# Reading x of the first three batches through column-tiled matmuls as it was loaded, with a new order of the loading phase

## The chip, the cores and the metric

The kernel runs on one core of a Trainium2 chip. The metric is the device time of one execution in microseconds (us); the median over several runs is compared. Engines, as the profile names them: PE is the matrix engine (TensorE, with PEld for its weight loads), DVE is VectorE, ACT is ScalarE, POOL is GpSimd, SP is SyncE, which here only issues DMAs. Each engine works through its own instructions in the order in which the program gives them.

## The reference

There are 8 batches of 8 heads, with 512 token rows and 32 state rows of 64 features. Tokens attend to the states and the states attend to the tokens; the 544 rows of each batch then go through a gated feed-forward block (512 to 1536 to 512).

```python
scores  = scale * x @ state.T ;  a  = exp(scores - max);  a  /= a.sum(-1) + 1e-9
xread   = a @ state                                   # for the 512 token rows
scores2 = scale * state @ x.T ;  a2 = exp(scores2 - max); a2 /= a2.sum(-1) + 1e-9
sread   = a2 @ x                                      # for the 32 state rows
y = concat([xread, sread], rows) ; heads side by side: 4352 x 512
out = (sigmoid(y @ w_gate) * (y @ w_val)) @ w_out     # float32
```

## The kernel before

One exponential table per batch, `E1` (128 token rows by 4 token groups c by 2 by 4 heads by 32 states), serves both directions. For the tokens, `n_sum`/`n_sums` and `n_mul`/`n_muls` divide it by its sum over the states, and its transpose `aT` (by `aT_mm` on PE for batches 0 and 1, by DMA later) is the moving operand of the block's first products. `xread` is never formed: the weights are first multiplied by the states (`sw_visit`, `sw_wide`: eight small matmuls at once on 64x32 tiles of the array, one per head, into PSUM, then `sw_cp` casts them to the SBUF tile `SW`), and `gv_mm(b, f)` multiplies `SW` by `aT` for one slice f of 128 of the 1536 hidden columns, gate and value half in a PSUM buffer each. `gv_th` (tanh on ACT) and `gv_glu` (product on DVE) form the gated slice and free those buffers; `out_mm(b, k)` sums four of twelve slices into 128 output rows.

For the states, `at_Eb` casts `E1` to bf16 (`Eb`, on POOL), and x is multiplied by it. Two ways of doing this exist. In batches 0 to 2 `sr_mm` (line 252) takes x in token order (`xb`, cast by `cast_x`) as the stationary operand, 16 matmuls of 64 columns; the sums over tokens come from eight matmuls with `ones` in batch 0, and in batches 1 and 2 from sums folded ahead by `p_tok`, `n_add` and `p_fold` and one matmul with `pick`; `sr_fin` divides and writes `XS`, the state rows of the block. In batches 3 to 7 `rd_mm` (line 285) takes `Eb` as stationary operand, 32 columns a head, four heads side by side on column tiles of the array, and `xs`, a copy of x with a column of ones, as the moving one: 32 matmuls of 65 columns; `rd_fin` divides and `rd_dma` transposes the result into `XS` by a DMA on SP. The block on the state rows of all batches, b = 8, comes last, from about 194 us on.

Loading: batch 0 comes partly as float32 (`load_xp`, then cast) and partly cast to bf16 by the DMA (`load_xh`, tile `xh`); batch 1 as `xh`; batches 2 on as float32. `load_w(w, lo, n)` loads columns lo to lo + n of the gate (0) or value (1) weights, cast on the way, `load_wo` the output weights, `load_sb` two batches of states. These go through POOL's queue. `xT_mm`/`xT_cp` transpose x for the scores `S_mm`, `S_exp` takes the exponential. `warm` issues matmuls whose result nobody reads.

PSUM has eight buffers: `GV` two, `SWP` four, `OU` one, `AT` one; a buffer is taken again when its last reader is done. The order of all calls is written out by hand (`manual_schedule`): lines 477 to 733 are the loading phase, in which batches 0 and 1 are worked through as their inputs and weights land; the loop at line 734 then treats batch b with the output of b - 1 and the preparation of b + 1.

Of the kernel before, what the change touches and what calls it, by code (L numbers as in the profile page):

```python
# [16 lines left out]
def kernel(  # L17
# [36 lines left out]
    ones = wp.tile((128, 2, 128), BF, name="ones")  # L54
# [192 lines left out]
    def sr_parts(b):  # L247
        ps = held["sr", b]
        return (ps[:, 0:256].rearrange("p (j e n) -> p j e n", j=4, e=2),
                ps[:, 256:384].rearrange("p (j n) -> p j n", j=4))  # L250

    def sr_mm(b, place):
        Eb = Ebs[b]
        held["sr", b] = place[0].tile((128, 512), FP, name="srp", tag=place[1])
        sr, sm = sr_parts(b)
        if ("hl", b) in held:
            nc.tensor.matmul(sm, pick, held["hl", b], start=True, stop=True)
            terms = []
        else:
            terms = [(e, Eb[:, c, e]) for e in range(2) for c in range(4)]  # L260
        for i, (e, rhs) in enumerate(terms):
            nc.tensor.matmul(sm, ones[:, e], rhs, start=(i == 0), stop=(i == len(terms) - 1))
        for j in range(4):
            for c in range(4):
                nc.tensor.matmul(sr[:, j], xbs[b][:, c, 2 * j:2 * j + 2].rearrange("p h d -> p (h d)"),  # L265
                                 Eb[:, c, :, j], start=(c == 0), stop=(c == 3))

    def sr_inv(b):
        r2 = held["r2", b] = ap_.tile((128, 4, Ns), FP, name="r2")
        nc.vector.reciprocal(r2, sr_parts(b)[1])  # L270

    def sr_fin(b):
        if ("r2", b) not in held:
            sr_inv(b)
        sr, r2 = sr_parts(b)[0], held["r2", b]
        for e in range(2):
            rows = slice(e * 64, (e + 1) * 64)
            nc.vector.tensor_tensor(XS[rows, b], sr[rows, :, e], r2[rows], ALU.mult)

# [5 lines left out]
    def rd_mm(b):  # L285

        ps = AT[0].tile((128, 512), FP, name="rdp", tag=AT[1])
        rd = held["rd", b] = ps[:, :2 * D + 2].rearrange("p (e d) -> p e d", e=2)
        for e in range(2):
            for c in range(4):  # L290
                for j in range(4):
                    nc.tensor.matmul(rd[j * Ns:(j + 1) * Ns, e], Ebs[b][:, c, e, j], xs[:, c, 2 * j + e, :D + 1],  # L292
                                     start=(c == 0), stop=(c == 3))
# [91 lines left out]
    def out_mm(b, k, place=None):  # L385
# [431 lines left out]
```

## Time and profile before

| | |
|---|---|
| median of 3 runs | 223.96 us (223.51 to 224.49) |
| the profiled execution | 224.5 us, span of its instructions 222.7 us |
| mean granted clock | 0.992 |
| PE busy | 213.9 us (96% of the span) |
| DVE, ACT, POOL busy | 123.5, 129.2, 66.6 us |
| `gv_mm` (L363), `out_mm` (L394) on PE | 96.5 and 95.9 us |
| HBM read, written | 18.35 and 8.91 MB |

The page splits the span in 40 slices of 5.57 us; a digit is a busy share in tenths. A timeline row gives start, length, engine, line, operation, output and inputs, the shape, the number of instructions merged, and in brackets how long the engine sat idle before and what ended it. The chain of waits follows the work that ended last back to what released it; its rows give start and length.

### The profile page before, as it was taken

What the parts mean: (1) busy time and instruction counts of PE and PEld (TensorE: products, weight loads), DVE (VectorE), ACT (ScalarE), POOL (GpSimd) and SP (SyncE); (2) the same over time, 40 slices, a digit from 0 to 9 for tenths busy, and PEclk for the clock granted to TensorE, in tenths of its full rate; (3) what the DMA queues carried; (4) which work ended last, traced back from release to release, by engine and by line L of the source; (5) the groups of instructions that cost most, each with busy time, mean ns of one, the idle gap of its engine ahead of it and who ended that gap; (6) DMA issues with size and microseconds to landing.
All of it is one profiled execution on the core that took longest, in us unless ns stands there. A gap on an engine that the chain in (4) does not pass through costs nothing.

```text
span 222.7 us, 4790 instructions
## 1 busy us (share of the span) xinstructions
PE 213.9 (96%) x1839; PEld 107.4 (48%) x1862; DVE 123.5 (55%) x214; ACT 129.2 (58%) x243; POOL 66.6 (30%) x124
## 2 busy tenths in 40 slices
PE   8679999999999999999999999999999999999994
PEld 3554444544444444444444444444444444466744
DVE  3599989986467445744484448354754334422301
ACT  3398797627675667656674866666756444433311
POOL 6699498556341036001800072003200000000001
PEclk9799999999999999999999999999999999999999
DMA  6999996984598349924552206421122111211114
GB/s 152 158 202 248 244 177 106 151 224 132 134 260 260 61 74 281 199 47 142 169 149 69 101 0 97 130 70 45 47 74 77 49 50 53 66 69 49 50 29 113
DMA packets 40982, 26.75 MB, mean 120 GB/s; under 512 B 23456, under 2 KB 36768, under 8 KB 40960
## 3 DMA queue, kind: packets, MB, share of 16 engines
q1 hardware_dynamic: 31088, 18.33, 31.6%
q0 software_dynamic: 9584, 7.93, 21.1%
q8 instruction: 14, 0.23, 0.4%
q10 hardware_dynamic: 288, 0.20, 0.3%
q14 instruction: 8, 0.07, 0.1%
HBM read 18.35 MB, written 8.91 MB: 122 GB/s over the span
## 4 chain that ended last, share of the span: by engine, by line
PE 90%; ACT 3%; DMA 3%; DVE 1%; issue 1%; POOL 0%; POOLq 0%
PE outp L394 38%; PE gvp L363 37%; PE swp L311 5%; PE gvp L366 5%; DMA xf<-in_x_dram 3%; PE Sp L152 1%; PE outp L416 1%; ACT E L157 1%; DVE SW L349 1%; PE rdp L292 1%; ACT xT L134 1%; PE xTp L131 0%; ACT aT L241 0%; ACT SW L349 0%; PE srp L265 0%
## 5 line engine op out<-in xcount | busy, mean ns | idle before, releaser
L378 DVE SCALAR_TENSOR_TENSOR glu<-th,gvp 128x512 bf16<-128x512 f32 (+1 forms) x108 | 70.1, 656 | 79.0 <-ACT th L373 63.5
L394 PE MATMUL outp<-wo,glu 128*128 128x512 bf16 x373 | 95.9, 379 | 1.3 <-issue 0.2
L363 PE MATMUL gvp<-aT,SW 128*128 128x512 bf16 x384 | 96.5, 379 | 0.5 <-ACT aT L241 0.5
L373 ACT ACTIVATE th<-gvp 128x512 f32<-128x512 f32 (+1 forms) x108 | 61.9, 576 | 59.3 <-PE gvp L363 45.8
L394 PEld LDWEIGHTS <-glu 128*128 128x128 bf16 x396 | 37.8, 98 | 41.9 <-issue 0.4
L363 PEld LDWEIGHTS <-SW 128*128 128x128 bf16 x384 | 36.2, 98 | 45.1 <-issue 4.2
L349 ACT CAST SW<-swp 128x512 bf16<-128x512 f32 x70 | 39.0, 586 | 4.3 <-PE swp L311 3.5
L398 ACT ACTIVATE res<-outp 128x512 f32<-128x512 f32 x33 | 19.7, 597 | 17.7 <-PE outp L394 17.7
L103 POOL COPY pre<-th 128x1 f32<-128x1 f32 x5 | 0.9, 188 | 69.0 <-ACT th L373 69.0
L407 POOL DMA_DIRECT2D out_dram<-res x2 | 1.1, 537 | 59.7 <-ACT res L398 59.7
L349 DVE CAST SW<-swp 128x512 bf16<-128x512 f32 x26 | 17.2, 684 | 2.9 <-PE swp L311 2.9
L163 POOL CAST Eb<-E 128x256 bf16<-128x256 f32 x32 | 12.0, 418 | 10.9 <-ACT E L157 10.9
L115 POOL CAST xb<-xf 128x1024 bf16<-128x1024 f32 x11 | 11.2, 1041 | 4.0 <-DMA xf<-in_x_dram 3.2
L157 ACT ACTIVATE E<-Sp 128x512 f32<-128x512 f32 x16 | 9.6, 604 | 3.3 <-PE Sp L150 2.8
L283 POOL CAST xs<-xf 128x1024 bf16<-128x1024 f32 x10 | 10.2, 1044 | 0.0
L311 PE MATMUL swp<-wg,sTc 64*32 64x512 bf16 (+1 forms) x192 | 8.7, 327 | 0.0
L170 DVE TENSOR_REDUCE rs<-E 128x16 f32<-128x512 f32 x12 | 8.2, 680 | 0.5 <-ACT E L157 0.4
L224 DVE TENSOR_TENSOR ab<-E,ri 128x512 bf16<-128x512 f32 x11 | 8.2, 742 | 0.0
L311 PE MATMUL swp<-wv,sTc 64*32 64x512 bf16 (+1 forms) x192 | 7.5, 322 | 0.0
L311 PEld LDWEIGHTS <-sTc 64*32 64x32 bf16 x384 | 4.9, 91 | 5.2 <-issue 3.0
L366 PE MATMUL gvp<-XS,wg 128*128 128x256 bf16 x48 | 7.2, 273 | 0.0
L366 PE MATMUL gvp<-XS,wv 128*128 128x256 bf16 x48 | 7.2, 273 | 0.0
(88 smaller groups left out, 129.0 us busy)
## 6 DMA issues: line engine op xcount, KB each, us to landing
out_dram<-res SPq DMA_DIRECT2D x27, 256.0 KB, 3.2
xf<-in_x_dram SPq DMA_DIRECT2D x4, 1024.0 KB, 6.6
xf<-in_x_dram POOLq DMA_DIRECT2D x2, 1024.0 KB, 7.5
wo<-in_moe_w_out_dram POOLq DMA_DIRECT2D x3, 512.0 KB, 5.6
out_dram<-res SPq DMA_DIRECT2D x9, 128.0 KB, 1.9
wg<-in_moe_w_gate_dram POOLq DMA_DIRECT2D x2, 512.0 KB, 9.3
wv<-in_moe_w_val_dram POOLq DMA_DIRECT2D x2, 512.0 KB, 10.4
xf<-in_x_dram POOLq DMA_DIRECT2D x3, 256.0 KB, 6.6
```

Source lines behind the costliest of these rows:

```text
L115: cp(xbs[b].rearrange("p c h d -> p h c d")[:, lo:lo + n], (xhs if b in xhs else xfs)[b][:, lo:lo + n])
L157: nc.scalar.activation(E1s[b][:, :, :, 2 * i:2 * i + 2].rearrange("p c e j n -> p (c e) j n"), held["S", b, i].rearrange("p c e j n -> p ( ...
L163: nc.gpsimd.tensor_copy(Ebs[b][:, c], E1s[b][:, c])
L283: pool(xs.rearrange("p c h d -> p h c d")[:, lo:lo + n, :, :D], xfs[b][:, lo:lo + n])
L311: nc.tensor.matmul(pss[e][j * Ns:(j + 1) * Ns, o:o + n], sTc[rows, b, j] if b > 1 else sTd[rows, b, 2 * j + e, e], (wg, wv)[w][rows, j, lo ...
L349: cp(*sw_left.pop((b, lo, w, e)))
L363: nc.tensor.matmul(ps, SWs[b][:, g, w, fs], aTs[b][:, :, g], start=(g == 0), stop=(g == 1))
L366: nc.tensor.matmul(ps, (wg, wv)[w][:, j, fs], XS[:, :, j], start=(j == 0), stop=(j == 3))
L373: nc.scalar.activation(th, held["gv", b, f][0], AF.Tanh, scale=0.5)
L378: nc.vector.scalar_tensor_tensor(glus[b][:, f], held["th", b, f], 1.0, held["gv", b, f][1], ALU.add, ALU.mult)
L394: nc.tensor.matmul(ops[b, c], glus[b][:, f, c * 128:(c + 1) * 128], wo[:, f], start=(f == 0), stop=(f == NF - 1))
L398: nc.scalar.activation(res, ops[b, c], AF.Copy, scale=0.5)
```

## The change

`sr_mm`, `sr_fin`, `sr_inv`, `p_fold`, `p_tok`, `n_add` and the tile `pick` go. `rd_mm` serves all batches: for batches 0 to 2 its moving operand is x as it was loaded (`xh` in batches 0 and 1, `xb` in batch 2), 64 columns, and 32 further matmuls of one column with a tile of ones give the sums. Its PSUM buffer is now named by the caller. The casts of batches 0 and 1 to token order go with that. The result tile `xr` has four buffers, and the three `rd_dma` of batches 0 to 2 are issued in the loop at b = 2, f = 8. Output rows of batch 6 are stored in halves for the last group only. `warm` has a tile of its own, filled with zeros. The loading phase is ordered anew: other PSUM buffers, other engines for some casts and copies, another order of the loads (x of batch 1 ahead of all weights; the weight columns 512 to 1023 ahead of 0 to 255; x of batch 2 after all of them), and three `gv_mm` of batch 1 just ahead of the loop.

```diff
-ones = wp.tile((128, 2, 128), BF, name="ones")
+ones = wp.tile((128, 1), BF, name="ones")
+wm = wp.tile((128, 128), BF, name="wm")
...
-def rd_mm(b):
+def rd_mm(b, place):
...
+                h, o, Eb = 2 * j + e, rd[j * Ns:(j + 1) * Ns, e], Ebs[b][:, c, e, j]
+                if b > 2:
+                    nc.tensor.matmul(o, Eb, xs[:, c, h, :D + 1], start=(c == 0), stop=(c == 3))
+                else:
+                    xh = xhs[b][:, h, c] if b in xhs else xbs[b][:, c, h]
+                    nc.tensor.matmul(o[:, :D], Eb, xh, start=(c == 0), stop=(c == 3))
+        if b < 3:
+            for c in range(4):
+                for j in range(4):
+                    nc.tensor.matmul(rd[j * Ns:(j + 1) * Ns, e, D:], Ebs[b][:, c, e, j], ones, start=(c == 0), stop=(c == 3))
...
-    xr = held["xr", b] = ap_.tile((128, 2, D), BF, name="xr")
+    xr = held["xr", b] = ap_.tile((128, 2, D), BF, name="xr", bufs=4)
...
-            n = 256 if 4 * (B - 1) - 4 <= 4 * b + c < 4 * (B - 1) else 512
+            n = 256 if 4 * (B - 1) - 1 <= 4 * b + c < 4 * (B - 1) else 512
...
+            if b == 2 and f == 8:
+                for q in range(3):
+                    rd_dma(q)
```

The new order of the loading phase, cut:

```diff
+nc.vector.memset(wm, 0.0)
+warm(2, AT)
+warm(1, SWP)
+load_s(0, nc.scalar)
+warm(4, GV)
+load_xp(0, nc.sync, 0, 2)
+make_identity(nc, ident)
+warm(1, OU)
+warm(2, GV)
+load_xh(0, 4, 4)
+zero(sTd, vec)
+cast_xp(0, vec, 0, 2)
+cast_s(0, vec)
+xT_mm(0, 0, GV)
+sT_mm(0, GV)
+sT_pad(1, act)
+xT_cp(0, 0, vec)
+sT_pad(0, vec)
+load_xh(1, 0, 4)
+load_xp(0, nc.sync, 2, 2)
+cast_xp(0, act, 2, 2)
+xT_mm(0, 1, SWP)
+S_mm(0, 0, GV, (0,))
+xT_cp(0, 1, vec)
+S_mm(0, 0, OU, (1,))
+S_exp(0, 0)
+xT_mm(0, 2, GV)
+xT_cp(0, 2, vec)
+load_xh(1, 4, 4)
+xT_mm(0, 3, OU)
+load_w(0, 256, 256)
+xT_cp(0, 3, act)
+S_mm(0, 1, OU, (0,))
+S_mm(0, 1, GV, (1,))
+load_w(1, 256, 256)
+S_exp(0, 1)
+xT_mm(1, 0, GV, 2)
+n_sum(0, 0)
+zero(sbz, vec)
+load_w(0, 1024, 512)
+n_sum(0, 1)
+load_w(1, 1024, 512)
+n_mul(0, 0, pool)
+xT_cp(1, 0, act, 2)
+xT_mm(1, 2, OU, 2)
+at_Eb(0)
+n_mul(0, 1, vec)
+S_mm(1, 0, GV)
+S_exp(1, 0)
+xT_cp(1, 2, vec, 2)
+aT_mm(0, SWP)
+aT_cp(0, 0, act)
+nc.vector.memset(ones, 1.0)
+S_mm(1, 1, SWP)
+load_sb(1)
+S_exp(1, 1)
+sw_visit(0, 256, 256)
+aT_cp(0, 1, vec)
+sw_cp(0, 256, 2, 0, act)
+load_w(1, 512, 512)
+sw_cp(0, 256, 2, 1, vec)
+sw_visit(1, 256, 256)
+warm(2, OU)
+at_Eb(1)
+load_sb(3)
+n_sums(1)
+gv_mm(0, 2, SWP)
+gv_th(0, 2)
+gv_glu(0, 2)
+gv_mm(0, 3, GV)
+sw_cp(1, 256, 2, 1, act)
+load_sb(2)
+rd_mm(0, OU)
+gv_th(0, 3)
+n_muls(1, vec)
+gv_glu(0, 3)
+load_w(0, 512, 512)
+sw_cp(1, 256, 2, 0, act)
+sw_visit(1, 1024, 512, 0)
+sw_cp(1, 1024, 0, 0, act)
+sw_visit(0, 1024, 512, 0)
+sw_cp(0, 1024, 0, 1, act)
+sw_cp(0, 1024, 0, 0, act)
+aT_mm(1, GV)
+rd_mm(1, AT)
+sw_visit(0, 1024, 512, 1)
+sw_cp(1, 1024, 0, 1, act)
+load_w(1, 0, 256)
+aT_cp(1, None, vec)
+sw_cp(0, 1024, 1, 1, vec)
+sw_cp(0, 1024, 1, 0, act)
+sw_visit(1, 1024, 512, 1)
+sw_cp(1, 1024, 1, 1, vec)
+gv_mm(0, 8, GV)
+gv_th(0, 8)
+gv_glu(0, 8)
+gv_mm(0, 11, SWP)
+nc.gpsimd.memset(xs[:, :, :, D:], 1.0)
+rd_fin(1)
+sw_cp(1, 1024, 1, 0, act)
+gv_mm(1, 2, SWP)
+gv_th(0, 11)
+rd_fin(0)
+load_w(0, 0, 256)
+gv_th(1, 2)
+gv_glu(0, 11)
+gv_mm(1, 9, GV)
+gv_th(1, 9)
+gv_glu(1, 2)
+sw_visit(0, 512, 512, 1)
+sw_cp(0, 512, 1, 0, act)
+gv_glu(1, 9)
+gv_mm(1, 3, SWP)
+gv_mm(0, 10, GV)
+sw_cp(0, 512, 1, 1, vec)
+gv_th(1, 3)
+sT_mm(1, AT)
+gv_th(0, 10)
+sT_cp(1, act)
+gv_glu(1, 3)
+sw_visit(0, 512, 512, 0)
+sw_visit(1, 512, 512, 0)
...
+gv_glu(0, 10)
+sw_cp(0, 512, 0, 0, act)
+load_x(2, nc.gpsimd)
+load_wo(1)
+gv_mm(1, 11, GV)
+sT_mm(2, AT)
+sw_cp(1, 512, 0, 0, act)
+sT_mm(3, OU)
+sw_cp(0, 512, 0, 1, vec)
+sw_visit(0, 0, 256)
+sw_cp(1, 512, 0, 1, vec)
+sw_visit(1, 512, 512, 1)
+gv_th(1, 11)
+gv_glu(1, 11)
+sw_cp(0, 0, 2, 0, act)
+gv_mm(0, 4, GV)
+gv_th(0, 4)
+sw_cp(0, 0, 2, 1, vec)
+sw_cp(1, 512, 1, 0, act)
+sw_cp(1, 512, 1, 1, vec)
+gv_mm(0, 5, SWP)
+gv_glu(0, 4)
+load_wo(0)
+gv_th(0, 5)
+gv_mm(0, 1, GV)
+gv_glu(0, 5)
+gv_th(0, 1)
+gv_glu(0, 1)
+load_wo(2)
+cast_x(2, vec, 0, 4)
+sT_cp(3, act)
+gv_mm(0, 6, SWP)
+cast_x(2, act, 4, 4)
+at_xT_dma(2)
+gv_mm(1, 7, SWP)
+gv_th(0, 6)
...
+zero(sTz, vec)
+pad(2, 6)
+S_mm(2, 0, GV)
+S_mm(2, 1, GV)
+S_exp(2, 0)
+S_exp(2, 1)
+out_mm(0, 11)
+load_x(3, nc.gpsimd)
+gv_mm(1, 10, GV)
+at_Eb(2)
+gv_glu(1, 5)
+n_sums(2)
+sw_wide(2, 0)
+n_muls(2, vec)
+aT_dma(2)
+gv_th(1, 10)
+out_mm(0, 1, GV)
+out_mm(0, 3)
+gv_glu(1, 10)
+sw_cp(2, 0, 0, 0, vec)
+sw_cp(2, 0, 2, 1, act)
+cast_x(3, vec, 0, 4)
+sw_cp(2, 0, 1, 1, act)
+sw_cp(2, 0, 0, 1, act)
+sw_cp(2, 0, 2, 0, act)
+sw_cp(2, 0, 1, 0, act)
+out_mm(0, 5)
+out_mm(0, 6, GV)
+sw_visit(1, 0, 256)
+rd_mm(2, GV)
+sw_cp(1, 0, 2, 0, act)
+sw_cp(1, 0, 2, 1, vec)
+sw_wide(2, 1)
+cast_x(3, pool, 4, 4)
+at_xT_dma(3)
+nc.scalar.activation(pre[:, 0:1], ones, AF.Exp)
+out_mm(0, 8)
+sw_cp(2, 1, 2, 1, act)
+sw_cp(2, 1, 1, 0, act)
+sw_cp(2, 1, 2, 0, act)
+gv_mm(1, 1, SWP)
+gv_th(1, 1)
+rd_fin(2)
+sw_cp(2, 1, 1, 1, vec)
+gv_glu(1, 1)
+sw_cp(2, 1, 0, 1, vec)
+out_mm(0, 10)
+gv_mm(1, 4, SWP)
+load_x(4, nc.sync)
+sw_cp(2, 1, 0, 0, vec)
+gv_th(1, 4)
+gv_glu(1, 4)
+gv_mm(1, 0, GV)
+gv_th(1, 0)
+gv_glu(1, 0)
+gate(xTs[2][:, 0, 3, 0:1])
```

More of the change, by code (lines that the diff above doesn't have):

```diff
@@ L245, in aT_dma @@
             nc.sync.dma_start_transpose(aT_tile(b)[:, c], abs_[b][:, c].rearrange("p e k -> p (e k)"))
[L247 to L278, printed above, removed]
     def cast_xs(b, lo, n):
         pool(xs.rearrange("p c h d -> p h c d")[:, lo:lo + n, :, :D], xfs[b][:, lo:lo + n])
-    def rd_mm(b):
-        ps = AT[0].tile((128, 512), FP, name="rdp", tag=AT[1])
+    def rd_mm(b, place):
+        ps = place[0].tile((128, 512), FP, name="rdp", tag=place[1])
         rd = held["rd", b] = ps[:, :2 * D + 2].rearrange("p (e d) -> p e d", e=2)
@@ L596 @@
+    gv_glu(0, 11)
[6 more added lines that the diff above has]
+    gv_mm(1, 3, SWP)
     gv_mm(0, 10, GV)
+    sw_cp(0, 512, 1, 1, vec)
+    gv_th(1, 3)
+    sT_mm(1, AT)
     gv_th(0, 10)
-    sw_visit(0, 0, 256)
-    sw_cp(0, 0, 2, 1, act)
-    gv_glu(0, 10)
-    sw_cp(0, 0, 2, 0, act)
-    sw_visit(1, 0, 256)
-    sw_cp(1, 0, 2, 0, vec)
-    sT_mm(2, AT)
-    gv_mm(0, 9, GV)
-    gv_mm(1, 9, SWP)
-    gv_th(0, 9)
@@ L608 @@
-    sw_cp(1, 0, 2, 1, act)
-    load_sb(3)
-    gv_th(1, 9)
-    cast_x(2, vec, 0, 4)
-    gv_mm(1, 11, SWP)
-    gv_glu(0, 9)
-    gv_glu(1, 9)
-    gv_mm(1, 0, GV)
-    sw_visit(0, 512, 512, 0)
-    zero(pick, pool)
+    sT_cp(1, act)
[11 more added lines that the diff above has]
+    sw_cp(0, 512, 0, 1, vec)
@@ new lines @@
+    at_xT_dma(2)
+    gv_mm(1, 7, SWP)
+    gv_th(0, 6)
+    gv_th(1, 7)
+    gv_glu(0, 6)
+    gv_mm(0, 0, GV)
+    gv_th(0, 0)
+    gv_glu(0, 0)
+    gv_mm(0, 7, SWP)
+    gv_th(0, 7)
+    gv_glu(0, 7)
+    gv_mm(1, 8, SWP)
+    gv_th(1, 8)
+    gv_glu(1, 8)
+    gv_mm(1, 6, GV)
+    gv_glu(1, 7)
+    gv_mm(0, 9, SWP)
+    gv_th(0, 9)
+    out_mm(0, 7, OU)
+    gv_mm(1, 5, SWP)
+    gv_th(1, 6)
+    out_mm(0, 0, GV)
+    gv_glu(0, 9)
+    gv_th(1, 5)
+    out_mm(0, 2)
+    sT_cp(2, act)
+    out_mm(0, 4)
```

252 lines of the change are left out of this document (4 added, 248 removed).

## The prediction

> **What bounds the kernel now.** I read the page's 40 slices first: PE is busy in nearly all of them.
>
> ```profile
> PE   8679999999999999999999999999999999999994
> PEclk9799999999999999999999999999999999999999
> DMA  6999996984598349924552206421122111211114
> ```
>
> Only the first three slices (to 16.7 us) have much idle PE, and the clock dips there alone. So the change can win time by an earlier start of dense work, by fewer PE cycles, or by fewer holes. The chain of waits in time order, cut to 0 to 21.5 us, says what paces that start:
>
> ```profile
> 1.47 6.61 DMA xf<-in_x_dram
> ...
> 8.12 0.61 PE xTp L131 x4
> ...
> 9.62 0.60 ACT E L157
> 10.22 0.48 ACT xT L134
> ...
> 11.18 0.60 ACT E L157
> 11.78 0.50 ACT xb L115
> 12.28 0.99 ACT xT L134
> 13.27 1.10 ACT E L157 x2
> 14.37 0.26 ACT sTc L459
> 14.63 0.49 ACT aT L241
> 15.12 0.98 ACT SW L349 x2
> ...
> 16.64 0.61 PE gvp L363 x2
> ```
>
> After the first x lands (8.08 us), ScalarE's queue is the path to the first `gv_mm`, with an `xb` cast (0.50) and the `sTc` copy (0.26) in it. Next, PE's timeline shows what the two ways of reading x cost:
>
> ```profile
> 15.15 0.63 PE L265 MATMUL srp<-Eb,xb 128*128 128x64 bf16 x16
> 20.84 5.41 PE L363 MATMUL gvp<-aT,SW 128*128 128x512 bf16 x24
> 57.09 1.04 PE L363 MATMUL gvp<-aT,SW 128*128 128x512 bf16 x4
> 68.02 0.42 PE L292 MATMUL rdp<-xs,Eb 128*32 128x65 bf16 x32
> 68.37 0.44 PE L311 MATMUL swp<-wg,sTc 64*32 64x512 bf16 x8
> ```
>
> The third line is `gv_mm(2, 0)`, the first product of the block loop, which the change hardly touches. Its start, 57.09, is my yardstick. Between 16.64 and 57.09 PE is busy 39.94 of 40.45 us, so from 20.84 on only the amount of PE work counts, unless the new order opens holes. Last, clock and weights:
>
> ```profile
> 7.00:8.00 1.00, 0.00 (x0) 0.00 (x0) 0.00 (x0) 0.32 (x1) 1.00 (x2) 1.00 1.28 168
> 8.00:9.00 1.00, 0.88 (x11) 0.88 (x12) 0.45 (x1) 0.00 (x0) 1.00 (x2) 0.50 1.20 135
> 19.70 0.27 PEld L311 LDWEIGHTS <-sTd 64*32 64x32 bf16 x9 [0.42 <-DMA wv<-in_moe_w_val_dram]
> 25.54 1.04 POOL L115 CAST xb<-xf 128x1024 bf16<-128x1024 f32 x1 [3.18 <-DMA xf<-in_x_dram]
> ```
>
> In the windows by time (columns: length, PE, PEld, DVE, ACT, POOL busy, clock, DMA share, GB/s) PE does nothing from 6.2 to 8.1 us and the granted clock is then 0.50 until 11.4. The two waits give landings: the fourth large weight piece at 19.65, x of batch 2 at 25.5.
>
> **Part 1, up to the first gv_mm (now 16.64).** The first x lands at 8.08 as before, being issued in the same place. I follow the new order queue by queue with the durations of before: four transposes 0.22 to the next issue and 0.40 to the result, an `xT` copy 0.42 on DVE and 0.58 on ACT (1.01 for a double one), S 0.40, exp 0.60, with 0.50 from one ACT instruction to the next in a row of them (seven took 3.73). `S_exp(0,0)` no longer waits for x heads 4 to 7: it starts near 8.1, not 9.62. Then, at full clock, `xT_cp(0,3)` 8.8, `S_exp(0,1)` 9.8, `xT_cp(1,0)` 10.4, `S_exp(1,0)` 11.8, `aT_mm(0)` 12.5, `S_exp(1,1)` 13.6, SW copies 14.1, `sw_visit(1,256)` 14.25, the two fill matmuls, first gv_mm 15.0. At half clock the same walk gives 15.6. So minus 1.6 or minus 1.04. The removed ACT casts (0.50) and the moved `sTc` copy are the larger part.
>
> Which clock: PE lost it after 1.9 us without work and kept it over 0.9 (12.4 to 13.3). The new order leaves it idle for 1.4 us at most (5.5 to 6.9, waiting for the second x cast, which ACT now does behind `sT_pad`). This lies between the rows. I take the full clock, since three more matmul groups fall into 6.9 to 8.1. The Trainium skill (TensorE: Matmul & The Clock Gate, Part 1) puts the loss at an idle window of about 3.4 us. By it the clock would stay full too (minus 1.6), but this trace lost it after 1.9, so the rule decides nothing here.
>
> **Part 2, from there to the dense run (16.64 to 20.84, 4.20 us).** New PE work: two gv_mm 1.73 (0.216 a matmul), `aT_mm` 0.44, four weight visits 0.9, two `rd_mm`, and some 0.4 for entering and leaving tiled stretches (0.16 in, 0.10 out, from the gaps at 26.2 and 30.8). An `rd_mm` of before is 0.35 on the chain. For batches 0 to 2 it gets 32 more matmuls of one column for the sums. No row has such matmuls. Bounds: nothing (only columns count, 1 of 65), or 0.35 again. Below nothing is excluded, as instructions are only added. I take 0.35, because each has its own weight load and the 32 loads of L292 alone take 0.30. So 0.70 each. The Trainium skill (TensorEngine Tiling, Instruction Overhead) says that a matmul of free size 1 takes as long as one of 60, which speaks against the change: by it `rd_mm` is 0.70, by columns 0.36, so three of them differ by 1.0.
>
> That is 4.87. ACT holds it up further: six SW copies, three tanh in one row from 16.2 (15.6 at full clock), each 0.50. The last value-weight visit waits for a PSUM buffer that `sw_cp(1,1024,0,1)` empties some 4.5 us after that. I get 5.5 us, plus 1.3. DVE's `n_muls(1)` (1.25) and the Eb casts on POOL end before their readers.
>
> **Part 3, from the dense run to gv_mm(2, 0) (36.25 us).** Same 22 gv_mm, 12 out groups, visits and wide visits. Out go two `sr_mm` (0.53 each: 0.47 and the pick matmul 0.06). In come `rd_mm(2)` 0.70 and `sT_mm(1)` 0.23, which moves here. There is one tiled stretch fewer (minus 0.26). Sum minus 0.4. No hole is added if covers hold: I followed each gv_mm to its buffers, at 0.50 a step on ACT and 0.60 on DVE (five gated products took 3.06). Tightest are the value buffers of `gv_mm(1,3)` and `gv_mm(0,10)`, and `sw_wide(3,0)` at the end, whose last buffer comes free with `gv_glu(1,4)` within 0.1 us of its use. If that cover fails, each DVE step late costs 0.6. DVE loses `n_add`, reciprocals of 0.95, XS products of 0.59 and three casts of x, and gains 0.45 for each `rd_fin` and half of x of batch 3 (0.83, POOL's now). ACT gains half of x of batch 2 (1.2, twice its 0.62 for half that size): queued behind it are the tanh of `gv_mm(0,6)` and `gv_mm(1,7)`, and `gv_mm(0,7)` waits for their buffers, with 0.4 us in hand by my walk; if x of batch 2 (31.4 by the rates below) came after 33, each later us is lost whole. POOL loses `p_tok` and `p_fold` (10 us) that no one waited for: worth nothing by itself.
>
> **Edits at nothing.** Three more transposing DMAs on SP at f = 8 of batch 2 (1.18 each) delay that queue by 3.6 us near 76. It idles 84.1 to 86.0, and the transposes behind are wanted 5 us or more later. XS is read at 194. Uncovered they would cost up to 3.6. The halved output rows of batch 6 lie 20 us before the end. `x` of batch 3 is issued near 42.6 (43.1 now), so DVE's cast near 49 finds it landed. `xr` in four buffers: free.
>
> **Sum.** Minus 1.6, plus 1.3, minus 0.4 is minus 0.7 at full clock (at half, minus 1.04, plus 1.3, minus 0.4: about minus 0.15). The profiled execution took 224.5 (span 222.7 and 1.8 around it), which becomes 223.8. It stood 0.54 over the median of 223.96, so I forecast a median of 223.3, own range 222.5 to 224.1. A half per cent (1.1 us) is about what a measurement of this kernel can tell from no change.
>
> **Rivals.** *Weights land late (slower).* The new order puts the first 256 columns of both weights behind the 512 block, with both batches' state loads ahead. In slice 11 to 17 cast loads moved 202 GB/s. From 19.65, at that rate: value 512 block with one state piece 22.6, gate block with two 25.8, then 27.1 and 28.4 for the two first blocks, and x of batch 2 some 3.0 later (5.9 us from 19.65 to 25.54 less 2.9 for what came between). They are wanted near 24.0, 26.4 and 28.4 (`sw_visit(0,0,256)`). The last margin is nothing, and the decisive rate is thus about 200. At 170 the 8.75 us from 19.65 to 28.4 become 10.4, which leaves PE waiting for 1.6: 223.3 and 1.6 is 224.9. For it: DMA is 0.9 busy there. Against it: by 30.5 the kernel of before has used every one of these bytes and x of batch 2 as well, so the queue can be faster than 202.
>
> *The clock stays half (slower).* If PE enters 15.6 at 0.50 and needs 3.3 us to get it back, as from 8.1 to 11.4, half of that is lost: minus 0.15 plus 1.65, 225.5. For it: few matmuls between 12 and 15. Against it: the clock held there before with as few.
>
> *Light reads and a full start (faster).* If one-column matmuls hide behind the other tiles, `rd_mm` is 0.36: 0.35 less in part 3 and as much in part 2, where ACT's row starts sooner. The two fill matmuls (0.43) are then the only cover still in the way. Minus 1.3 to minus 1.8, so 222.4. For it: PE work is all that counts after 20.84. Against it: the 0.30 of loads.
>
> *The change does little.* x was read in 2.1 us of PE work (1.02, 0.53, 0.53) and will be in 2.1 (3 of 0.70). If ACT takes back the start, 224.0. This is the forecast's own upper part.
>
> **How the numbers follow.** Forecast with its upper part 0.47 (of it 0.12 below 222.84, 0.34 within, 0.01 above). Light reads 0.24, all faster. Late weights 0.19 and half clock 0.10, all but 0.01 slower. Faster 0.36, same 0.35, slower 0.29. The range 222.0 to 225.5 leaves out a tenth at each end: a start better than walked, or late weights and half clock together.
>
> **What would show it.** First gv_mm near 15.0 (15.6 at half clock), the run from `gv_mm(0,8)` near 20.5 (21.1), `gv_mm(2,0)` near 56.5. `rd_mm` of batch 0 lasts 0.7. No PE wait on DMA at the visits of 24 to 29. After 57 us both traces run in step. I am wrong if PE waits on a weight load or on an SW or glu step on DVE or ACT for more than 0.5 us after 21, if the clock reads 0.5 after 12 us, or if the block loop itself changes pace.

## The result, and the profile after

The kernel after takes 225.87 us (median of 4 runs, 225.75 to 226.37) against 223.87 (4 runs, 223.51 to 224.49) for the kernel before: a ratio of 1.0086, 95% interval 1.006 to 1.0112. It is slower by 0.9%, clear of the interval, and lies above the prediction's range of 222.0 to 225.5. Its profiled execution took 226.37 us with a span of 224.6.

The slices of the page after:

```profile
PE   8599999999989999999999999999999999999994
PEclk9859999999999999999999999999999999999999
DMA  6999999892597243994643304521122111121113
```

Two things differ from before: the clock's third slice (11.2 to 16.8 us) is at half, and PE's twelfth (61.8 to 67.4 us) is no longer full. The chain of waits after, cut to the first 22 us (start, length, what):

```profile
7.66 0.41 PE xTp L132 x4
...
8.91 0.60 ACT E L158
9.50 0.49 ACT xT L135
...
10.62 0.87 PE xTp L132 x8
...
11.51 1.02 ACT xT L135
...
13.18 0.97 PE aTp L197 x8
...
14.76 0.51 ACT E L158
...
15.94 0.76 PE warm L369 x2
16.70 1.73 PE gvp L302 x8
```

`S_exp(0,0)` starts at 8.91 instead of 9.62, and from there PE itself is on the chain with long rows: eight transposes take 0.87 and 0.97 us, and the two fill matmuls 0.76, all at half clock. The first `gv_mm` gains nothing worth speaking of. The windows after say when the clock was lost (columns: length, PE, PEld, DVE, ACT, POOL busy, clock, DMA share, GB/s):

```profile
6.10:9.50 3.40, 1.49 (x28) 1.04 (x22) 1.70 (x4) 1.79 (x4) 0.91 (x2) 1.00 1.42 191
9.50:13.00 3.50, 2.72 (x32) 2.56 (x32) 3.27 (x8) 2.09 (x4) 2.33 (x4) 0.50 1.37 201
13.00:16.50 3.50, 3.31 (x54) 2.05 (x52) 2.29 (x5) 2.20 (x4) 3.29 (x8) 0.52 1.26 206
```

It fell to half at 9.5, when PE had been busy for 1.49 of 3.40 us, and came back at 16.4. PE's timeline after, for the hole ahead of the loss, for the new reads and the yardstick, and for the place in the loop where PE is not full:

```profile
7.66 0.40 PE L132 MATMUL xTp<-ident,xf 128*128 128x128 bf16 x4 [1.32 <-ACT xf L91]
...
16.54 1.89 PE L302 MATMUL gvp<-aT,SW 128*128 128x512 bf16 x8
18.36 0.30 PE L228 MATMUL rdp<-xf,Eb 128*32 128x64 bf16 x16
18.48 0.25 PE L232 MATMUL rdp<-ones,Eb 128*32 128x1 bf16 x16
18.59 0.32 PE L228 MATMUL rdp<-xf,Eb 128*32 128x64 bf16 x16
18.72 0.30 PE L232 MATMUL rdp<-ones,Eb 128*32 128x1 bf16 x16
18.95 0.73 PE L250 MATMUL swp<-wg,sTd 64*32 64x512 bf16 x16
...
21.86 0.82 PE L302 MATMUL gvp<-aT,SW 128*128 128x512 bf16 x3
...
57.79 1.04 PE L302 MATMUL gvp<-aT,SW 128*128 128x512 bf16 x4
...
61.25 0.25 PE L153 MATMUL Sp<-sTz,xT 128*128 128x64 bf16 x3
62.38 0.32 PE L153 MATMUL Sp<-sTz,xT 128*128 128x64 bf16 x5 [0.88 <-DMA xT<-xb]
...
69.77 0.42 PE L225 MATMUL rdp<-xs,Eb 128*32 128x65 bf16 x32
```

The dense run starts 1.02 us later than before (21.86), the yardstick `gv_mm(2, 0)` 0.70 later (57.79), `rd_mm(3)` 1.75 later (69.77). The last step is a wait: `S_mm(3, 0)` does three matmuls at 61.25 and then stands 0.88 us for the transposes of x of batch 3. Their queue, SP's timeline, first before and then after:

```profile
45.57 5.03 SPq L245 DMA_TRANSPOSE aT<-ab  x4
50.70 1.01 SPq L402 DMA_DIRECT2D out_dram<-res  x2
53.69 5.13 SPq L139 DMA_TRANSPOSE xT<-xb  x4
```

```profile
48.82 6.41 SPq L211 DMA_TRANSPOSE aT<-ab  x4
55.32 0.52 SPq L341 DMA_DIRECT2D out_dram<-res  x1
55.95 5.17 SPq L140 DMA_TRANSPOSE xT<-xb  x4
```

In the kernel after the scores of batch 2 come later, `aT_dma(2)` starts 3.25 us later and holds the queue 1.38 us longer, and the transposes of x of batch 3, next but for an output row, start 2.26 us later. From `gv_mm(3, 0)` on, at 71.08 us (69.17 before), the difference is constant, and the last products start at 218.90 (217.00 before).

### The profile page after: what moved, and what is told of

It reads as the page before. It is cut to its first block, busy times and chain, and to the rows that moved or that the text cites. A ratio compares the mean times of both kernels' runs of the same rounds, so it can differ in the third digit from the quotient of the medians.

```text
span 224.6 us, 5038 instructions
## 1 busy us (share of the span) xinstructions
PE 216.8 (97%) x1996; PEld 108.5 (48%) x1996; DVE 119.4 (53%) x206; ACT 129.1 (57%) x242; POOL 52.1 (23%) x88
## 3 DMA queue, kind: packets, MB, share of 16 engines
HBM read 18.35 MB, written 8.91 MB: 121 GB/s over the span
## 4 chain that ended last, share of the span: by engine, by line
PE 86%; SPq 5%; ACT 4%; DVE 3%; DMA 1%; issue 1%; DVEq 0%; ACTq 0%
PE gvp L302 35%; PE outp L333 34%; PE gvp L305 5%; PE swp L250 4%; SPq L211 3%; PE warm L369 2%; SPq L140 2%; PE Sp L153 1%; PE outp L355 1%; DMA xT<-xb 1%; ACT E L158 1%; ACT SW L288 1%; PE xTp L132 1%; ACT xT L135 1%; PE Sp L151 1%
## 5 line engine op out<-in xcount | busy, mean ns | idle before, releaser
L333 PE MATMUL outp<-wo,glu 128*128 128x512 bf16 x396 | 98.2, 379 | 0.0
L312 ACT ACTIVATE th<-gvp 128x512 f32<-128x512 f32 (+1 forms) x108 | 61.8, 575 | 58.3 <-PE gvp L302 45.2
L288 ACT CAST SW<-swp 128x512 bf16<-128x512 f32 x73 | 40.5, 587 | 6.2 <-PE swp L250 5.6
L288 DVE CAST SW<-swp 128x512 bf16<-128x512 f32 x23 | 15.5, 685 | 0.5 <-PE swp L250 0.5
L164 POOL CAST Eb<-E 128x256 bf16<-128x256 f32 x32 | 12.0, 416 | 11.2 <-ACT E L158 11.2
L116 POOL CAST xb<-xf 128x1024 bf16<-128x1024 f32 x9 | 10.1, 1151 | 5.2 <-DMA xf<-in_x_dram 3.1
```

What stands on the lines that cost most here:

```text
L116: cp(xbs[b].rearrange("p c h d -> p h c d")[:, lo:lo + n], (xhs if b in xhs else xfs)[b][:, lo:lo + n])
L164: nc.gpsimd.tensor_copy(Ebs[b][:, c], E1s[b][:, c])
L288: cp(*sw_left.pop((b, lo, w, e)))
L312: nc.scalar.activation(th, held["gv", b, f][0], AF.Tanh, scale=0.5)
L333: nc.tensor.matmul(ops[b, c], glus[b][:, f, c * 128:(c + 1) * 128], wo[:, f], start=(f == 0), stop=(f == NF - 1))
```

## The experiments

Ratios are against runs of the kernel before on the same chip, whose medians were 223.97 to 224.38 us; they are ratios of mean times, and so differ a little from those of the medians. Starts of stages come from one profiled execution of each kernel. `e1` and so on are the labels.

**Does the wait at `S_mm(3, 0)` cost the time?** `e1_s_later` takes it off the kernel after:

```diff
+d = 1 if nb == 3 else 0
-if f in (1, 2):
-    S_mm(nb, f - 1, AT); S_exp(nb, f - 1)
-if f in (2, 3):
-    n_sum(nb, f - 2)
+if f in (1 + d, 2 + d):
+    S_mm(nb, f - 1 - d, AT); S_exp(nb, f - 1 - d)
+if f in (2 + d, 3 + d):
+    n_sum(nb, f - 2 - d)
```

> The changed kernel, with S_mm(3,0) and S_mm(3,1), their exponentials and row sums one slice f later in the loop at b = 2, so that PE does not reach them before x of batch 3 is transposed. Theory Q (queue): the 1.05 us that the changed kernel loses between 60.4 and 62.5 us is only PE waiting for the last transposing DMA of x of batch 3, which stands behind the transposes of aT of batch 2 on SP's queue; without the wait the loop keeps pace with the kernel before from 58 us on, so 225.87 less 0.9 to 1.2 = 224.7 to 225.0, and PE's wait for DMA xT<-xb is gone. Rival: the shift is handed on (the table of batch 3 comes later, so n_mul, aT and the first gv_mm of batch 3 wait instead): 225.6 to 225.9.

Measured: 225.41 us (12 runs), ratio 1.004, 1.0017 to 1.0063. There is no wait left at that place, and `rd_mm(3)` follows `sw_wide(3, 0)` by 11.71 us as before (after: 12.76). The time lies between the theory and its rival: about half of the forecast gain, and the interval still overlaps that of the kernel after. `e11_before_late_x3` puts the lateness on the kernel before, by letting GpSimd do each of the two casts of x of batch 3 twice:

```diff
 cast_x(3, pool, 4, 4)
+cast_x(3, pool, 4, 4)
...
 cast_x(3, pool, 0, 4)
+cast_x(3, pool, 0, 4)
```

> The kernel before with each of the two casts of x of batch 3 on GpSimd done twice (some 2.1 us more on GpSimd, the result the same), so that the four transposes of x of batch 3 are issued some 2 us later (55.7 instead of 53.7, as in the kernel after), and nothing else is moved. Theory of the late transposes (that the kernel after loses its 1.05 us at S_mm(3, 0) because of when they start): TensorE waits 0.8 to 1.2 us there for the last of them, and the time is 224.7 to 225.3. Rival (what the kernel after loses comes of its loading phase, and the wait seen is its sign only): the transposes land in time or the wait is made up within the loop, and the time is 223.7 to 224.2.

Measured: 225.64 us (10 runs), ratio 1.0055, 1.0034 to 1.0076. SP's and PE's timelines of e11:

```profile
55.59 5.13 SPq L139 DMA_TRANSPOSE xT<-xb  x4
```

```profile
60.25 0.22 PE L152 MATMUL Sp<-sTz,xT 128*128 128x64 bf16 x2
60.66 0.20 PE L152 MATMUL Sp<-sTz,xT 128*128 128x64 bf16 x1 [0.18 <-DMA xT<-xb]
62.00 0.32 PE L152 MATMUL Sp<-sTz,xT 128*128 128x64 bf16 x5 [1.14 <-DMA xT<-xb]
```

Transposes issued 1.9 us later make PE wait 1.32 us and the kernel 1.3 us longer (a little over what the theory said), and ahead of the two casts nothing is changed. So the mechanism is shown: late transposes cost time by themselves. How much they cost the kernel after is less sure. e1 won only half of what it should, and the profiled execution of `e13_rows4`, the same kernel but for the size of three stores, lost only 0.29 us at that place.

```diff
-n = 256 if 4 * (B - 1) - 1 <= 4 * b + c < 4 * (B - 1) else 512
+n = 256 if 4 * (B - 1) - 4 <= 4 * b + c < 4 * (B - 1) else 512
```

> The kernel after with the rows of batch 6 stored in halves again, as in before (the bound 4 * (B - 1) - 4 instead of 4 * (B - 1) - 1). Theory (the larger stores of batch 6 cost nothing, 20 us before the end): 225.4 to 226.2, as after. Rival (they do hold the last stores up): 224.3 to 225.0.

Measured: 225.99 us (6 runs), ratio 1.0082, 1.0059 to 1.0104. `e15_before_rows1` makes the opposite edit in the kernel before.

> The kernel before with three of the four row blocks of batch 6 stored whole, as in the kernel after, and nothing else changed. Theory (no cost): within 0.3 us of before, 223.8 to 224.6. Rival (they hold the last stores up): 225.0 to 225.8, with the time after the last instruction on data longer by 1 us or more.

Measured: 224.20 us (12 runs), ratio 1.0007, 0.9992 to 1.0023. The stores cost nothing either way, so these two serve as second profiles of the kernels after and before, and of executions nearer to their medians (225.93 and 224.15 us):

| us, start of | before | e15 | after | e13 |
|---|---|---|---|---|
| mean clock | 0.992 | 0.999 | 0.985 | 0.982 |
| first `gv_mm` | 16.64 | 15.99 | 16.54 | 16.57 |
| dense run | 20.84 | 20.19 | 21.86 | 21.90 |
| `sw_wide(3, 0)` | 56.31 | 55.67 | 57.01 | 57.08 |
| `rd_mm(3)` | 68.02 | 67.38 | 69.77 | 69.08 |
| last products | 217.00 | 216.44 | 218.90 | 218.06 |

The profiled execution of before had lost its clock for 3.4 us, and e15's had not. Windows of the two, before first, with the 3.4 us ahead of that point:

```profile
4.60:8.00 3.40, 1.62 (x20) 0.80 (x17) 2.06 (x5) 1.68 (x3) 3.40 (x6) 1.00 1.30 163
8.00:11.40 3.40, 3.22 (x33) 2.74 (x34) 1.99 (x5) 1.29 (x3) 1.20 (x3) 0.50 1.34 152
```

```profile
4.60:8.00 3.40, 2.89 (x24) 1.46 (x22) 2.44 (x6) 1.33 (x3) 3.40 (x6) 1.00 1.26 144
8.00:11.40 3.40, 2.67 (x45) 2.02 (x43) 2.14 (x6) 2.31 (x5) 1.98 (x3) 1.00 1.51 178
```

Full clock is the rule for the kernel before: of its 109 runs beside the experiments, 85 had a mean clock of 0.998 or more (median 223.98 us) and 23 had 0.990 to 0.992 (median 225.07), so a mean clock as that of the profiled execution (0.992) goes with about 1.1 us more. For the new loading order half clock is the rule: of the 19 runs of after, e13 and e16 none was above 0.992, and of e1's twelve two were (224.58 and 224.90 us, the shortest and the third shortest; the other ten have a median of 225.44). Between e15 and e13, 1.71 us are lost by the start of the dense run (0.58 of it is there at the first `gv_mm`, and 1.13 come behind that), 0.30 come back by `sw_wide(3, 0)`, 0.29 go in the loop's first half and 0.08 come back behind it: 1.62, and 1.78 in the time.

**Does the clock cost the time?** `e2_fill` fills PE's holes in the kernel after with matmuls of no use.

```diff
 sT_mm(0, GV)
+warm(4, AT)
...
 S_mm(0, 0, GV, (0,))
+warm(2, AT)
...
 xT_mm(0, 3, OU)
+warm(3, AT)
...
 xT_mm(1, 2, OU, 2)
+warm(2, AT)
```

> The changed kernel with 4, 2, 3 and 2 more fill matmuls on the AT buffer in PE's holes of the first 13 us. Theory C (clock): the dense run starts at 21.86 and not near 20.5 because the clock is 0.50 from 9.5 to 16.4 us; with the holes filled the granted clock stays 1.00, first gv_mm near 15.2 to 15.6, gv_mm(0,8) near 20.4 to 20.9, time 224.7 to 225.1. Rival (ScalarE's row of casts and the buffers behind it set the start, whatever the clock): gv_mm(0,8) stays within 0.3 us of 21.86 and the time within 0.3 us of 225.87; if the fills themselves run at half clock, each costs 0.43 and the time rises by up to 1 us.

Measured: 226.62 us (6 runs), ratio 1.0125, 1.0092 to 1.0157: longer than theory and rival alike. The clock stays at 1.00 through the loading phase, the first `gv_mm` starts at 15.29 and the dense run at 20.87, 0.99 before that of after and 0.68 behind that of e15. Then PE's timeline of e2:

```profile
60.33 0.25 PE L153 MATMUL Sp<-sTz,xT 128*128 128x64 bf16 x3
62.59 0.32 PE L153 MATMUL Sp<-sTz,xT 128*128 128x64 bf16 x5 [2.01 <-DMA xT<-xb]
62.74 1.46 PE L333 MATMUL outp<-wo,glu 128*128 128x512 bf16 x4
```

PE comes 0.92 us earlier and waits until 62.59, and behind the wait the matmuls run at half clock (1.46 us for four). It looks as if the wait had taken the whole gain, but the queue was not late here. SP's timeline of e2, and how long these four transposes took from issue to landing:

```profile
54.46 5.16 SPq L140 DMA_TRANSPOSE xT<-xb  x4
```

```profile
DMA to landing us min/median/max: 2.4/2.5/4.2
```

They were issued 1.49 us earlier than in the kernel after, and the last of them, issued at 58.35, took 4.2 us to land instead of 2.5. At 2.5 x would have been there near 60.9 and the wait would have been about 0.3 us (an estimate from these rows). This execution, 228.25 us at a mean clock of 0.992, is also the slowest of the six; the other five had a clock of 1.00, and so no such half-clock stretch, and took 226.21 to 227.85. So the trace shows what one execution lost, not why the median is long. `e4_fill_s_later` is e2 and e1 together.

> The changed kernel with both edits, the fills and the later S of batch 3. If C and Q are two separate losses they add: 223.7 to 224.2. If both are one loss (an earlier start alone brings the transposes early enough), the time equals that of the fills alone within 0.3 us.

Measured: 225.71 us (9 runs), ratio 1.0073, 1.0045 to 1.0101. Neither forecast had this time. Beside the profile of before, its own shows nothing of either loss: dense run 20.90, `rd_mm(3)` 67.99, last products 217.14. But that profile had its half-clock stretch; beside e15, at full clock like e4, the dense run starts 0.71 us later and the last products 0.70. And that execution took 226.59. 2 us more lie at the very end, where one of the last stores took 3.6 us to land (2.4 at most in before). `e14_fill_s_later_rows4` adds e13's edit to it.

> e4_fill_s_later (matmuls of no use in the holes of the loading phase, S_mm(3, ...) one f later) with the rows of batch 6 stored in halves again. Theory (the size of these stores has no part in the late landing at the end): 225.2 to 226.0, as e4_fill_s_later, and last stores landing in up to 3.6 us in some executions. Rival (the whole rows delay the last stores): the landing at the end is 1.7 to 2.4 us as in before and the time is 223.8 to 224.5.

Measured: 226.33 us (6 runs), ratio 1.0091, 1.0066 to 1.0116. The last stores land in 2.1 us at most and the median is no shorter, so their size was not it. The profiled execution, 226.97 us, has a span of 224.1: 2.9 us lie outside it, against 1.8 in before. PE's timeline shows the wait one block on, at `S_mm(4, 0)`:

```profile
84.96 0.32 PE L153 MATMUL Sp<-sTz,xT 128*128 128x64 bf16 x5 [0.50 <-DMA xT<-xb]
```

The later scores of batch 3 send `aT_dma(3)` out later, and the transposes of batch 4 stand behind it on SP. So I moved batch 4's too (`e16_s34_later`, `d = 1 if nb in (3, 4) else 0`), then with the fill (`e17_fill_s34_later`), then every batch's (`e18_fill_s_all_later`, `d = 1`).

> The kernel after with S_mm, exp and n_sum of batches 3 and 4 one f later. Theory (what e1_s_later still lost in the loop is the wait for the transposes of batch 4, and the rest is the half clock of the loading phase): no TensorE wait on a DMA in the loop, rd_mm(3) to rd_mm(4) in 23.3 to 23.5 us, time 224.8 to 225.2. Rival (the lateness is handed on from block to block, since each later score sends the next aT_dma out later): a wait at S_mm(5, ...), or a time of 225.3 and more as in e1_s_later.

> The same with the holes of the loading phase filled by matmuls of no use (clock full). Theory (half clock and the two waits are the whole loss): time 223.9 to 224.6, level with before. Rival (the lateness is handed on): 225.3 to 226.3, as e4_fill_s_later and e14.

> The same with the scores of every batch of the block loop one f later. Theory: as e17_fill_s34_later, 223.9 to 224.6. Rival (handed on even so, or the added delay of aT_dma in each block opens waits of its own): 225.3 to 226.5, with waits on a DMA in later blocks.

Measured: 225.33 us (9 runs; 1.006, 1.0039 to 1.008), 225.65 (11 runs; 1.0072, 1.0044 to 1.0101) and 226.45 (6 runs; 1.0104, 1.0067 to 1.0141). All three times are those of the rival. PE's waits of e17 and of e18 behind the loading phase (sum, times, longest):

```profile
PE gvp L302 <- DVE glu L317: 0.4, 2, 0.2
```

```profile
PE gvp L302 <- DVE glu L317: 1.4, 5, 0.6
PE Sp L153 <- DMA xT<-xb: 0.3, 1, 0.3
```

The waits on the DMA go, and in their place VectorE's gated products come late, the more the more batches are moved. In e17 these waits are small. Its profiled execution (224.94 us) starts the dense run at 21.16, 0.97 us behind e15, reaches `sw_wide(3, 0)` 0.65 behind and the last products 1.03 behind: most of it is lost before the loop.

**Can the queue be put right at its root?** `e6_s2_early` brings the scores of batch 2 forward in the loading phase; `e7_fill_s2_early` adds the fill, `e8_fill_s2_spread` also moves the three new `rd_dma` apart.

```diff
 out_mm(0, 2)
+gate(xTs[2][:, 0, 3, 0:1])
+load_x(3, nc.gpsimd)
...
-S_mm(2, 0, GV)
-S_mm(2, 1, GV)
+S_mm(2, 0, SWP)
+S_mm(2, 1, SWP)
...
+out_mm(0, 4)
 at_Eb(2)
...
 aT_dma(2)
+out_mm(0, 11)
...
-if b == 2 and f == 8:       # e8 alone
-    for q in range(3):
-        rd_dma(q)
+if 3 <= b < 6 and f == 8:
+    rd_dma(b - 3)
```

> The changed kernel with the scores of batch 2 some 2.6 us earlier (sT_cp(2), zero(sTz) and pad moved up, S_mm(2,*) behind out_mm(0,2) on SWP, n_sums, n_muls and aT_dma(2) with them) and x of batch 3 loaded as soon as x of batch 2 is transposed; the loop untouched. Theory Q (SP's queue): aT_dma(2) starts near 46, not 48.8, the transposes of x of batch 3 end before 60, the PE wait of 0.9 at S_mm(3,0) is gone and the time is 224.6 to 225.1. Rival (it is not the queue but something in the loop): the wait stays and the time is 225.6 to 226.0.

> e6 with the fills of e2. Theory C and Q together: full clock from 5 us on, gv_mm(0,8) near 20.9, sw_wide(3,0) near 56.0, no wait for x of batch 3: 223.5 to 224.1, 0.7 to 0.9 less than e6. Rival (an earlier start only brings PE sooner to the same transposes, as in e2): no better than e6.

> e7 with the three rd_dma of batches 0 to 2 in the loops at b = 3, 4 and 5, one each, in place of all three at b = 2. If three transposes at once delay SP's queue so that x of batch 4 or 5 comes late, this is 0.2 to 0.5 faster than e7; if the queue has room, as the prediction says, equal to e7 within 0.2.

Measured: 225.84 us (10 runs; 1.0073, 1.0042 to 1.0104), 226.22 (10 runs; 1.0098, 1.0067 to 1.0129), 226.51 (6 runs; 1.0098, 1.0065 to 1.0131). In all three `rd_mm(3)` follows `sw_wide(3, 0)` by 11.71 us, as before, so the wait in the loop is gone, as theory Q said; the times of e6 and e7 are still those of the rivals. `sw_wide(3, 0)` itself comes at 57.47, 58.49 and 57.79. In e7 it follows the start of the dense run by 37.46 us (after: 35.15), and PE's waits between 22 and 72 us show 1.4 of these 2.3 us:

```profile
PE Sp L153 <- DMA xT<-xb: 0.6, 3, 0.2
PE swp L250 <- DVE glu L317: 0.5, 1, 0.5
PE swp L250 <- DMA wg<-in_moe_w_gate_dram: 0.3, 1, 0.3
```

The earlier scores wait for the transposes of batch 2, and a gated product is late. Spreading the `rd_dma` changed nothing that can be measured; `e12_before_3dma` prices them alone, by issuing three more transposing DMAs at that place in the kernel before.

```diff
+if b == 2 and f == 8:
+    for q in range(3):
+        rd_dma(3)
```

> The kernel before with three more transposing DMAs of the same size as the new ones on SyncE's queue at f=8 of loop b=2: rd_dma(3) is issued three more times there (the same data to the same place); nothing else is changed. Theory (they cost nothing, as the prediction had it, since nobody on the way to the end waits for what lies behind them): within 0.3 us of before, 223.8 to 224.6, and every later stage starts within 0.1 us of before against the start of its loop. Rival (three more transposing DMAs on that queue are dear in themselves, by what they delay on it or at the landing of the last stores, and are the rest of what e4_fill_s_later and e10_before_rd0 lose with no wait on TensorE to show for it): 224.9 to 225.6.

Measured: 224.38 us (12 runs), ratio 1.0011, 0.999 to 1.0032. They cost nothing that can be measured.

**Is it the order or the reads?** `e3_before_rd` keeps the order of before, and takes only the new reads: `rd_mm` for `sr_mm` of batches 0 to 2, without the casts of batches 0 and 1, `p_tok`, `p_fold`, `n_add` and `pick`.

```diff
-cast_x(0, ...), cast_x(1, ...), p_tok(1), p_fold(1), n_add(2), p_fold(2), pick
...
-sr_mm(0, OU)
+rd_mm(0, OU)
...
-sr_fin(0)
+rd_fin(0)
```

> The kernel before, in its own order, with rd_mm in the places of the three sr_mm: the column-tiled reads alone, casts of x of batches 0 and 1, sum folding and pick gone, the three rd_dma in the loop. Theory O (the new order costs, the reads do not): rd_mm takes 0.6 for sr_mm's 1.0, 0.53, 0.53 and ScalarE's path to the first gv_mm is one cast of 0.5 shorter, so 223.2 to 223.9. Rival (the reads cost: drains between tile modes, 32 loads more each): 224.4 to 225.4.

Measured: 226.16 us (6 runs), ratio 1.009, 1.0068 to 1.0113: the reads alone, in the old order, lose as much as the whole change, and more than even the rival had. The profile showed one loss. GpSimd's and then SP's timeline of e3:

```profile
26.86 1.65 POOL L106 DMA_DIRECT2D wo<-in_moe_w_out_dram  x2
```

```profile
28.30 6.92 SPq L139 DMA_TRANSPOSE xT<-xb  x4
```

GpSimd, rid of its casts and sums, issues `load_wo(1)` right behind `load_wo(0)` (before: at 35.46), beside the transposes of batch 2, which take 6.92 us (before 5.22); `S_mm(2, ...)` then waits 0.7. `e5_rd_gated` holds that load back by a gate on those transposes, `e9_rd_late_wo` by its place, behind `pad(2, 6)`.

```diff
-load_wo(1)
...
 at_xT_dma(2)
+gate(xTs[2][:, 0, 3, 0:1])    # e5
+load_wo(1)                    # e5
...
 pad(2, 6)
+load_wo(1)                    # e9
```

> The kernel before with rd_mm in place of sr_mm, as in e3, and one thing more: the second load of output weights waits on POOL until x of batch 2 is transposed (a one-element copy of that tile ahead of it), so that it is issued near 36 us, as before, and not at 27.7. Theory D (in e3 the folding that went from POOL had held that load back; issued 8 us sooner it slowed the transposing DMAs of x of batch 2, 6.92 us for four instead of 5.22, and PE waited for them): S_mm(2,0) has no wait left, so only the reads remain: about 0.17 us each at the places of batches 1 and 2, less 0.1 from the start, 224.0 to 224.5. Rival (the reads cost the 2 us of e3): 225.5 to 226.3.

> The order of before, with the one-column-tiled matmuls for batches 0 to 2 and without the casts (as in e3_before_rd), but load_wo(1) moved to just behind pad(2, 6) in GpSimd's program, so that it cannot start in the middle of the transposes of x of batch 2; no added gate. Theory (what e3_before_rd lost at S_mm(2, ...) and behind came of the early load of wo(1), which GpSimd issued at 26.9 us instead of 35.5 once its casts were gone): the transposes of x of batch 2 take 5.2 to 5.4 us again, S_mm(2, ...) waits for none of them, the start of gv_mm(2, 0) comes back to 57.0 to 57.5, and the time is 224.0 to 224.6. Rival (the matmuls themselves cost more than the casts gave back, wherever the load lies): the time stays at 225.5 to 226.3 as in e3_before_rd, with no wait on a DMA to see at S_mm(2, ...).

Measured: 226.93 us (5 runs; a sixth took 229.92; 1.0113, 1.008 to 1.0147) and 226.46 (6 runs; 1.0088, 1.0054 to 1.0123). The transposes are back to 5.40 and 5.28 us, as the theory said, but no time is won. e5 says little about the total, since its gate sent `pad` out late:

```profile
PE Sp L152 <- POOL sTz L408: 1.9, 1, 1.9
```

In e9 `S_mm(2, ...)` waits for nothing, and still the time is the rival's: the load was a cost seen in e3's trace, but without it the loss stays. e9's profiled execution, at 225.50 us the fastest of its six, starts the dense run 0.92 us behind e15 (21.11) and the last products 1.18 behind (217.62). `e10_before_rd0` takes the new read for batch 0 alone, in the order of before.

```diff
-cast_x(0, ...)    # four casts
-sr_mm(0, OU)
+rd_mm(0, OU)
-sr_fin(0)
+rd_fin(0)
+rd_dma(0)         # b == 2, f == 8
```

> The order of before, with the new column-tiled matmuls for batch 0 alone: the four casts of batch 0 into token order (three on VectorE, one on ScalarE, 6 to 15 us) go, the sums and sr_mm of batches 1 and 2 stay, and the one extra transposing DMA of the result is issued in loop b=2 at f=8. GpSimd's program is as in before, and so are the times at which it starts its loads. Theory (the casts of batch 0 lie beside waits for the weights, and rd_mm(0) costs 0.6 us against 0.4 for sr_mm(0)): within 0.3 us of before, 223.7 to 224.3; the dense run starts at 20.5 to 21.0. Rival (the casts of batch 0 do hold the loading phase): the dense run starts under 20.3 and the time is 223.0 to 223.5, faster than both kernels.

Measured: 225.80 us (8 runs), ratio 1.0058, 1.0036 to 1.008. Neither theory held. PE's timeline of e10, at full clock:

```profile
14.23 0.30 PE L319 MATMUL swp<-wg,sTd 64*32 64x256 bf16 x8 [0.89 <-DMA wg<-in_moe_w_gate_dram]
...
16.31 1.02 PE L371 MATMUL gvp<-aT,SW 128*128 128x512 bf16 x4 [0.74 <-ACT aT L241]
...
21.09 0.61 PE L371 MATMUL gvp<-aT,SW 128*128 128x512 bf16 x2
```

PE waits longer for x (2.2 us in sum up to 21 us against 0.5 in e15), and for a weight load that e15 did not wait for, and the dense run starts at 21.09, 0.90 behind e15. The read itself is cheaper: `rd_mm(0)` takes 0.59 us (from 14.57), `sr_mm(0)` with its sums takes 1.02 in e15 (from 14.25). Why the loads of this kernel and of e3 and e9 land late again and again is open: one profile of each cannot tell.

No version beat the kernel before. Open as well is what the filled kernels lose beyond their traces: at full clock e4's nine runs reach from 224.34 to 227.02 us, before's full-clock runs (beside e16) from 223.41 to 224.47. The fill brought the clock back and no time: the medians with it are, if anything, longer, by 0.75 us (e2 and after), 0.30 (e4 and e1), 0.39 (e7 and e6) and 0.32 (e17 and e16). One part of it lies outside the span of the instructions: in 26 of the 54 runs of the seven kernels with the fill the time is 1.86 to 3.04 us above the span, in none of 210 other runs is it more than 1.85. Why is not shown.

## Why the prediction was wrong, point by point

**Part 1 failed, at "I take the full clock".** The hole on which it hung was there nearly as walked (1.32 us, waiting for ScalarE's cast of x; 1.4 foretold), and the three matmul groups behind it as well, but the clock did not survive: half from 9.5 to 16.4 us. The first `gv_mm` came at 16.54, not at 15.0; even the half-clock walk (15.6) was 0.9 us too early. Of this 0.8 were there while the clock was still full: `S_exp(0,0)` started at 8.91, not near 8.1, since the cast of x on which the hole waits ended on ScalarE at 7.61 and not at 6.9. At full clock the walk was 0.3 to 0.8 short (first `gv_mm` at 15.29 to 15.78 in the seven kernels with the fill).

**"It stood 0.54 over the median, so I forecast a median of 223.3" was the second failing step.** The profiled execution stood over the median because of its half-clock stretch: e15, at full clock, has its dense run 0.65 us earlier. The walk compared a full-clock start after with a half-clock start before, and then took off 0.54 once more. Against e15 the prediction's own 20.5 for the dense run is a loss of 0.3; with part 3 the sum should have been about nothing. The profiles at full clock show the same: the kernels with the fill reach the first `gv_mm` 0.2 to 0.7 us before e15 (15.99), not 1.6, while part 2 costs them 1.1 to 1.5 (5.33 to 5.75 us against 4.20), so their dense run starts 0.7 to 1.1 us later. The gain of 1.6, the largest term of the sum, was mis-sized even at the clock that it assumed.

**Part 2 held**: 5.32 us (foretold 5.5) from the first `gv_mm` to the dense run, 5.33 to 5.75 with the fill. The `rd_mm` were mis-sized only a little: 0.59, 0.59 and 0.66 us for 0.70. Sixteen matmuls of one column take 0.11 us on PE's timeline (18.48 to 18.59), nearly as long as sixteen of 64 columns (0.12 to 0.13), so the choice of the upper bound was near the mark, and light reads are out.

**Part 3 held**: 35.93 us from the dense run to `gv_mm(2, 0)` against 36.25, a gain of 0.32 (0.4 foretold). No cover failed: PE waited for no SW or glu step and for no weight load, so the late weights did not happen.

**"After 57 us both traces run in step" failed.** I had followed every PSUM buffer but not SP's queue. In "Edits at nothing" only the three new `rd_dma` and x's landing were weighed; that the scores of batch 2 move to 44.20 (39.99 before), and with them `aT_dma(2)`, on whose queue the transposes of batch 3 stand next, was not. It cost 1.05 us in the profiled execution, 0.29 in e13's. The three `rd_dma` themselves are free, as foretold (e12). So are the rows of batch 6 (e13, e15).

**Of the rivals**, the half clock came true and its figure, 225.5, was the nearest, but partly by luck: the clock was back at 16.4, just ahead of the first `gv_mm`, so nothing was lost to it behind that, and the time is made of a later start and the wait in the loop, not of the two terms that it summed.

**The clock.** The kernel after lost it with no hole longer than 1.32 us. What the losses share is that PE was busy for less than half of the 3.4 us ahead: 1.49 and 1.68 of 3.40 us in after and e13, 1.62 in before, against 2.89 in e15 and 3.05 in e2, which kept it there. It came back after a stretch with 3.22, 3.31 or 3.03 us of work (before, after, e13), not after 2.72 or 2.21. The share alone does not settle it: e10 kept the clock over 11.0 to 14.4 us with 1.64 us of work. The half-clock stretches lasted 3.4, 6.8 and 6.8 us (before, after, e13). The Trainium skill (TensorE: Matmul & The Clock Gate, Part 1) has a free-running window of about 3.4 us; one and two windows agree with these lengths. Its condition for a loss, an idle window, does not agree: these windows were nearly half busy. If the clock is decided window by window, e10 need not speak against a share, since its stretch can lie across two windows: cut from 3.06 us on, its four stretches of 3.41 us hold 2.92, 2.00, 1.96 and 1.78 us of work. Which share decides stays open.

## What to carry to other kernels

Before taking a profiled execution as the base of a sum, look whether its own clock is that of the median run; a forecast at full clock must be set against a profile at full clock. When steps are re-ordered, walk every in-order queue past them, those that only issue DMAs above all: a transfer's place on the queue can decide a wait two stages later. And look where the profiled execution stands among its runs before reading a cause from it: e2's was the slowest of six and showed a late landing, e9's the fastest.

## What the runs showed of the hardware

Work taken off GpSimd made TensorE wait, since GpSimd issues loads: in e3 `load_wo(1)` came 8 us earlier, four transposing DMAs beside it took 6.92 us instead of 5.22, and PE waited 0.7 us for them; with the load held back they took 5.40 and 5.28 (e5, e9). A transposing DMA can also land late by itself: in e2 the last of four landed 4.2 us after its issue, while the median was 2.5. And PE lost its clock to half in the middle of a running kernel, after a single wait of 2.01 us (e2, 60.6 to 62.6 us): the four matmuls behind it took 1.46 us instead of 1.03, and the clock was back 3.4 us after it fell.
